# Fused Fourier mixing and maxout feed-forward: the order of the first loads, two-engine casts, a column fetched through DRAM, and where the last scatter stores are issued

## The chip, the cores and the metric

The kernel runs on one core of one Trainium2 chip. The metric is the device time of one execution in microseconds (us); the time given for the kernel is the median of several runs. A core has five engines with an instruction stream each: PE (TensorE, the matrix unit), DVE (VectorE), ACT (ScalarE), POOL (GpSimd) and SP (SyncE, which here only issues DMAs). They run side by side and wait for each other on semaphores. Matmuls write to PSUM, which is divided into banks; DVE and ACT read PSUM and copy ("evict" or "cast") its content to SBUF, where the operands of the next matmul lie. [...]

## The reference, cut to what matters

```
def _attn_ref(x):                       # x: 8 x 3072 x 256, float32
    X = np.fft.fft(x, axis=1)
    X = np.fft.fft(X, axis=2)
    return X.real

def _moe_ref(x, w1, w2, w3, w_out):     # 24576 tokens, d_model 256, d_ff 768
    h = np.maximum(np.maximum(x @ w1, x @ w2), x @ w3)
    return h @ w_out
```

The output is `_moe_ref(_attn_ref(x))`, 24576 x 256 in float32.

## The kernel before, in words

The transform along the sequence is split in two steps (one of 32 points, one of 96 points), the transform along the features is folded into the weights: tables `md` and `nmd` of cosines and sines are multiplied with the weights (`product`, L303), which gives `g_all` and, as differences, `gd_all`. Half of the feature range follows from the other half by symmetry, so each unit of work computes a "plus" and a "minus" result from the same operands.

**Stages of one batch** (class `Mix`, L383). `load_x` (L116) brings rows of x into `xt` by a DMA on POOL's queue that also casts to bf16; h = 0 is the first half of the rows, h = 1 the mirrored ones. `mirror` (L123) fills partitions 64 to 127 with the features in reverse order, on DVE for batch 0, plus one strided copy of a single column. `s(k)` (L392) is the first transform step for eight of the 49 rows (k = 6 is the last row alone) and casts the PSUM result into `tb`. For batch 0, `t` (L428) transposes `tb` into `yb` on DVE; later batches go through DRAM instead (`y`, `z`, L414 and L421, on SP). `k` (L456) is the second step; its casts give `tE` and `tO`, the operands of everything after. For block 0 of batch 0 `tE` is cast by DVE and `tO` by ACT.

**Units.** Each batch has 18 units: three blocks of 512 tokens times six column groups `jc` of d_ff. `begin` (L852) and `finish` (L869) compute one unit. A normal unit needs four matmuls and casts both halves; a "split" unit (odd ones from the 7th on, and those in `EXTRA`) has its third product computed ahead by `third` (L837): two matmuls, an ACT copy `odd`, a DVE operation `even` that adds `vb` times the column `wcol`, and on POOL two sums `plus` and `minus` (L850). DVE then takes the maxima (L862, L874). `l2_block` (L553) multiplies the hidden values with `w_out` and adds a linear part; `l2_last` (L584) does it for the last block, and stores as it goes.

**Stores.** The plus half of a block is stored by SP (`stores_plus`). The minus half goes out by indirect DMAs from POOL; they wait in the list `waiting`, and `scatter(n)` (L649) issues n of them at fixed units: one at units 8, 10 and 12 and two at unit 14, the rest at the end (L904, L919). They share POOL's queue with the sums.

**The order of the work** is written out by hand: nothing moves except by its place in the program. L672 to L725 are the head, before the first unit; `plan` (L754 to L820) gives what is put behind each unit of the main loop (L880). [...]

**What the change touches.** `FIRST` (L147) are the row ranges in which batch 0 is loaded: 0 to 16, 16 to 32, 32 to 40, 40 to 49. The loads stand behind six index ramps on POOL (L149 to L157). The cast of `s(5)` (L690) is one DVE copy. `column` (L345) makes `wcol`, one number per d_ff index, by 24 matmuls of one column and an ACT copy; it stands behind unit 5 (L797). The scatter pace is L904.

Of the kernel before, what the change touches and what calls it, by code (L numbers as in the profile page):

```python
# [9 lines left out]
FP32 = mybir.dt.float32  # L10
BF16 = mybir.dt.bfloat16
# [16 lines left out]


FIRST_OF = (4, 8, 1)  # L30
EXTRA, EXTRA_LAST = (0, 4, 8), (0, 4, 8, 14)


def _parts(g):

    done = [(12 + i - 1, slice(128 * i + 96, 128 * i + 128)) for i in range(4)]
    for i in range(4 if g < 2 else 3):
        done.append((FIRST_OF[g] + i - 1, slice(128 * i, 128 * i + 96)))
    if g == 2:
# [5 lines left out]
def kernel(  # L45
# [9 lines left out]
    nc = tc.nc  # L55

    B, S, D = x.shape
    assert (S, D) == (3072, 256)
    DFF = moe_w1.shape[1]
    NJC = DFF // 128  # L60
# [3 lines left out]
    NS = 49  # L64
# [6 lines left out]
    consts = ctx.enter_context(tc.tile_pool(name="consts", bufs=1))  # L71
    ps_f = ctx.enter_context(tc.tile_pool(name="ps_f", bufs=3, space=bass.MemoryType.PSUM))
    d_pool = ctx.enter_context(tc.tile_pool(name="dbuf", bufs=1, space=bass.MemoryType.DRAM))
    dbs = [d_pool.tile([NS, 64 * 128], BF16, name=f"db{i}", tag=f"db{i}") for i in range(2)]
    vds = [d_pool.tile([1, NHALF], BF16, name=f"vd{i}", tag=f"vd{i}") for i in range(2)]
    t_pool = ctx.enter_context(tc.tile_pool(name="tbuf", bufs=2))

    xt = [consts.tile([128, NS * 256], BF16, name=f"xt{i}", tag=f"xt{i}") for i in range(2)]
# [17 lines left out]
    md = [md_all[:, fc * 256:(fc + 1) * 256] for fc in range(2)]  # L96
    nmd = [nmd_all[:, fc * 256:(fc + 1) * 256] for fc in range(2)]
    w1_bf = consts.tile([128, 2 * DFF], BF16, tag="w1_bf")
    w2_bf = consts.tile([128, 2 * DFF], BF16, tag="w2_bf")
    w3_bf = consts.tile([128, 2 * DFF], BF16, tag="w3_bf")  # L100
    wout_bf = consts.tile([128, NJC * 256], BF16, tag="wout_bf")
    g1t = consts.tile([128, NJC * 256], BF16, tag="g1t")
    g_all = consts.tile([128, 4 * DFF], BF16, tag="g_all")
    g_all = g_all.rearrange("p (c k j) -> p c k j", k=4, j=128)
# [5 lines left out]
    mark = consts.tile([1, 1], FP32, tag="mark")  # L110
    sgn = consts.tile([128, 1], FP32, tag="sgn")
    wcol = consts.tile([128, NJC], FP32, tag="wcol")
    dif = consts.tile([128, 1], FP32, tag="dif")
    t_mid = consts.tile([128, 2, B], BF16, tag="t_mid")

    def load_x(b, s0, s1, h):  # L116

        rows = x[b].rearrange("(a s) d -> a s d", s=96)
        lo, hi = (s0, s1) if h == 0 else (max(s0, 1), min(s1, 48))
        src = rows[:, lo:hi, :] if h == 0 else rows[:, 97 - hi:97 - lo, :][:, ::-1, :]  # L120
        return nc.gpsimd.dma_start(out=xt[b % 2][32 * h:32 * h + 32, lo:hi, :], in_=src)  # L121

    def mirror(b, s0, s1):  # L123

        t = xt[b % 2]
        fn = (nc.vector.tensor_copy, (nc.gpsimd.tensor_copy, nc.vector.tensor_copy)[s0 >= 25],
              nc.scalar.copy)[min(b, 2)]
        fn(out=t[64:128, s0:s1, 1:128], in_=t[0:64, s0:s1, 255:128:-1])  # L128
        if b < 2:
            if b == 0 and s0 < 40:  # L130
                fn = nc.scalar.copy
            fn(out=t[64:128, s0:s1, 0], in_=t[0:64, s0:s1, 128])
# [8 lines left out]
    ps_s = ps_s_cm.__enter__()  # L141

    def iota(t, pattern, base=0, cm=0):
        nc.gpsimd.iota(t, pattern, base=base, channel_multiplier=cm,
                       allow_small_or_imprecise_dtypes=True)

    FIRST = ((0, 16), (16, 32), (32, 40), (40, NS))  # L147

    pidx = gen.tile([128, 1], FP32, tag="pidx")  # L149
    iota(pidx, [[0, 1]], cm=1)  # L150
    pidx_i = gen.tile([128, 1], INT32, tag="pidx_i")
# [18 lines left out]
            iota(kvec[:, NHALF:NHALF + 1], [[0, 1]], base=0)  # L170

    dvec = gen.tile([128, 128], FP32, tag="dvec")
    for c, (s0, s1) in enumerate(FIRST):
        for h in range(2):
            load_x(0, s0, s1, h)
        if c == 0:
            iota(dvec, [[1, 128]])
        elif c < 3:
            ramp(c - 1)

    def load_w(k, j0, j1):
# [74 lines left out]
    dve = nc.vector.tensor_copy  # L256
# [17 lines left out]
    def wrap(c0, c1):  # L274
# [3 lines left out]
    phase(512, 1024)  # L278
    mirror(0, *FIRST[0])
    turns(512, 1024)  # L280
    nc.vector.tensor_scalar(out=vm, in0=vm, scalar1=255, scalar2=None, op0=ALU.bitwise_and)
    nc.vector.tensor_copy(out=vm.rearrange("p (fc k c) -> p fc k c", fc=2, k=2)[:, :, :, 0],
                          in_=par.unsqueeze(1).to_broadcast([128, 2, 2]))
# [60 lines left out]

    def column():  # L345

        psc = ps_f.tile([128, 512], FP32, name="psc", tag="ps")
        for jc in range(NJC):
            for k, (table, wt) in enumerate(((md, w3_bf), (nmd, w1_bf))):
                for fc in range(2):  # L350
                    nc.tensor.matmul(psc[:, jc:jc + 1],
                                     wt[:, fc * DFF + jc * 128: fc * DFF + jc * 128 + 128],
                                     table[fc][:, 128:129],
                                     start=(k == 0 and fc == 0), stop=(k == 1 and fc == 1))
        nc.scalar.copy(out=wcol, in_=psc[:, 0:NJC])

    def prep_second():

# [290 lines left out]
    def scatter(n):  # L649

        for _ in range(min(n, len(waiting))):
            row, col, p0, p1, src = waiting.pop(0)
            stored(nc.gpsimd.indirect_dma_start(  # L653
                fours, bass.IndirectOffsetOnAxis(ap=rows_m[p0:p1, col:col + 1], axis=0),
                src, None, element_offset=256 * row), "scattered", ("scattered", "direct"))
            nc.gpsimd.memset(mark, 0.0)
# [11 lines left out]
    def warm_up(n):  # L668
        for _ in range(n):
            nc.tensor.matmul(warm, zero[:, 0:128], zero, start=True, stop=True)  # L670

    m = Mix(0)  # L672
# [8 lines left out]
    m.s(2, pool=ps_s)  # L681
    m.s(3, pool=ps_s)
    warm_up(1)
    mirror(0, *FIRST[3])
    m.s(4, pool=ps_s)
    warm_up(2)
    scal(sgn, pidx, 0.0, ALU.is_equal)
    scal(sgn, sgn, 2.0, ALU.mult, -1.0, ALU.add)
    scal(dif, sgn, 1.0, ALU.subtract)
    m.s(5, pool=ps_s, evict=dve)  # L690
    nc.scalar.activation(out=md_all, in_=vm, func=AX.Sin, scale=float(2.0 * math.pi / 256.0),
                         bias=turn[:, 0:1])
    m.s(6, pool=ps_s)
    m.t()
    warm_up(2)
# [6 lines left out]
    for (s0, s1) in HALVES:  # L702
        for h in range(2):
            load_x(1, s0, s1, h)
        if s0 == 0:
            nc.gpsimd.dma_start(out=wout_bf.rearrange("p (jc c) -> p jc c", jc=NJC),
                                in_=moe_w_out.rearrange("(jc p) c -> p jc c", jc=NJC))
# [8 lines left out]
    table(1, 512, 1024)  # L716
    m.c(1, 16)
    warm_up(1)
    m.k(0, 0, dve)
    m.k(1, 0)  # L720
    differ(0, 2, 0, 128)
    keep(psg2, 1, 2, 128, 384, dve)
    differ(0, 2, 128, 384)
# [21 lines left out]
    first, second = prep_first(), prep_second()  # L745
# [42 lines left out]
    for (u, fn) in ((0, lambda: table(2, 512, 1024)),   # L788
                    (0, lambda: next(second)), (0, lambda: next(first)),
                    (1, lambda: m.k(1, 1)), (1, lambda: next(second)), (1, lambda: next(first)),  # L790
                    (1, lambda: table(0, 512, 1024)),
                    (2, lambda: m.v(1)), (2, lambda: m.k(0, 1)), (2, lambda: next(first)),
                    (2, lambda: next(second)), (2, lambda: next(first)), (2, lambda: table(1)),
                    (3, lambda: m.c(16, RI)), (3, lambda: m.c(0, 1)),
                    (3, lambda: table(2)), (3, lambda: table(0)),
                    (4, lambda: m.k(1, 2)), (4, lambda: m.k(0, 2)), (4, m.end),
                    (5, rows), (5, column), (5, lambda: next(second)), (6, lambda: m.v(2))):  # L797
        at(0, u, fn)

    for ch in range(4):  # L800
# [79 lines left out]
    for g in range(B * UNITS):  # L880
        b, u = divmod(g, UNITS)
        blk, jc = divmod(u, NJC)
        mm = mixes[b]
        last = b == B - 1 and blk == 2
        if jc == 0:
            hp = h_pool.tile([128, NJC, TOKB], BF16, name="hp", tag="hp")
            hm = h_pool.tile([128, NJC, TOKB], BF16, name="hm", tag="hm")
            if last:
                flipped = []
                for t, name in ((mm.tE, "tEr"), (mm.tO, "tOr")):  # L890
                    fl = h_pool.tile([128, TOKB], BF16, name=name, tag=name)
                    flipped.append(fl)
                    nc.gpsimd.tensor_copy(fl, t[:, 3 * TOKB - 1: 2 * TOKB - 1: -1])
        if prev is not None and is_split(prev[0]) and not is_split(g):
            finish(*prev)
            prev = None
        pses = begin(g, hp[:, jc, :])
        if prev is not None:
            finish(*prev)
        prev = (g, pses, hm[:, jc, ::-1] if last else hm[:, jc, :])  # L900
        for lead in (1, 2):
            if is_split(g + lead) and (lead == 1) == (g + lead == 7):
                third(g + lead)
        scatter({8: 1, 10: 1, 12: 1, 14: 2}.get(u, 0))  # L904
        l2_some(10)
        if b == B - 1 and u in (1, 3):
            if u == 1:
                middle = l2_mid()
            next(middle, None)
        for fn in plan.get((b, u), ()):  # L910
            fn()
        if jc == NJC - 1:
            l2_some(1000)
            if g == B * UNITS - 1:
                finish(*prev)
            l2_queue.append(l2_last(hp, hm, mm.tE, mm.tO, flipped) if last else
                            l2_block(b, blk, hp, hm, mm.tE, mm.tO))
# [32 lines left out]
```

## Time and profile before

| what | value |
|---|---|
| median of 3 runs | 392.08 us (391.94 to 392.52) |
| the profiled execution | 391.42 us |
| span of its instructions | 389.3 us |
| mean granted TensorE clock | 0.998 |
| DMA, mean over the span | 139 GB/s |

The span runs from the first instruction to the last event of the core; 2.1 us of the profiled execution lie around it. The page has six parts: busy time by engine, the span in 40 slices, the DMA queues, the chain of work that ended last, the costliest groups, and the DMA issues. Busy time of PE counts the whole length of overlapping matmuls, so the chain and the waits, not the busy share, tell whether it is the bound. In the chain a piece stands with its start and its length, the engine, the tile and the line; in the timeline a row has start, length, engine, line, operation, output and input tiles, shape, count, and in brackets the idle time before and what ended it. Rows of the same form are merged, and "x18" is their number.

### The profile page before, as it was taken

The numbers are of one execution on the slowest core, as the hardware profiler recorded it, in microseconds if no ns is written. First come the engines' busy times: TensorE is split into PE (matmuls) and PEld (weight loads), VectorE is DVE, ScalarE is ACT, GpSimd is POOL, SyncE is SP. The second block draws the span as 40 slices with busy tenths as digits, with TensorE's granted clock in tenths as the row PEclk, the third lists the DMA queues.
The fourth block names the chain that finished last, engine by engine and source line by source line (L and its number), as shares of the span: only waits on it lengthen the run. The fifth ranks groups of instructions, "written<-read, shape, count | busy, mean of one in ns | idle before, by whom it ended". The sixth has DMA issues, their size and how long they took to land.

```text
span 389.3 us, 8092 instructions
## 1 busy us (share of the span) xinstructions
PE 376.2 (97%) x2817; PEld 236.2 (61%) x2817; DVE 327.7 (84%) x552; ACT 248.4 (64%) x453; POOL 314.3 (81%) x363
## 2 busy tenths in 40 slices
PE   6699999999999999999999999999999999999985
PEld 2355566566665666566665666656665666666654
DVE  7788797799797988899797988989887997999972
ACT  6877789567856696567856687567866346434420
POOL 9983576879898898879898898879787887769881
PEclk9999999999999999999999999999999999999999
DMA  7999764585747666475938657575423544212226
GB/s 113 184 183 160 163 145 118 112 168 161 178 141 130 172 176 154 111 128 186 189 120 149 169 151 176 125 128 185 113 94 93 149 138 139 70 31 80 85 89 206
DMA packets 52263, 54.13 MB, mean 139 GB/s; under 512 B 26547, under 2 KB 45009, under 8 KB 51367
## 3 DMA queue, kind: packets, MB, share of 16 engines
q0 software_dynamic: 20272, 26.45, 34.4%
q1 hardware_dynamic: 31418, 26.58, 25.0%
q10 hardware_dynamic: 532, 0.59, 0.5%
q8 instruction: 22, 0.36, 0.3%
q14 instruction: 19, 0.16, 0.1%
HBM read 36.95 MB, written 30.81 MB: 174 GB/s over the span
## 4 chain that ended last, share of the span: by engine, by line
PE 87%; POOL 4%; DVE 4%; DMA 2%; ACT 1%; issue 1%; DVEq 0%; POOLq 0%
PE po L549 30%; PE pse L492 10%; PE pse L860 5%; PE pse L485 5%; PE pse L486 5%; PE d L843 5%; PE e L841 5%; PE pse L861 5%; PE po L572 5%; PE ps L461 3%; PE ps L396 3%; PE pl L565 2%; DMA xt<-in_x_dram 2%; POOL xt L121 1%; POOL plus L850 1%
## 5 line engine op out<-in xcount | busy, mean ns | idle before, releaser
L850 POOL TENSOR_TENSOR plus<-even,odd 128x512 bf16<-128x512 f32 x91 | 115.7, 1271 | 55.4 <-DVE even L846 44.1
L850 POOL TENSOR_TENSOR minus<-even,odd 128x512 bf16<-128x512 f32 x91 | 115.5, 1269 | 0.0
L845 ACT ACTIVATE odd<-d 128x512 f32<-128x512 f32 x91 | 54.4, 598 | 55.8 <-PE d L843 41.9
L862 DVE SCALAR_TENSOR_TENSOR hp<-pse,plus 128x512 bf16<-128x512 f32 x91 | 62.6, 688 | 32.2 <-PE pse L861 27.9
L549 PE MATMUL po<-wout_bf,hp 128*128 128x256 bf16 x576 | 86.1, 273 | 0.0
L498 ACT ACTIVATE stmp<-pse 128x512 bf16<-128x512 f32 x106 | 63.2, 600 | 24.2 <-PE pse L486 11.2
L549 PE MATMUL po<-wout_bf,hm 128*128 128x256 bf16 x576 | 78.6, 273 | 0.0
L549 PEld LDWEIGHTS <-hp 128*128 128x128 bf16 x576 | 56.3, 98 | 26.2
L492 PE MATMUL pse<-tO,gd_all 128*128 128x512 bf16 x197 | 66.1, 380 | 1.3 <-DVE hp L862 1.3
L846 DVE SCALAR_TENSOR_TENSOR even<-vb,wcol,e 128x512 f32<-128x512 bf16 x91 | 67.1, 737 | 0.0
L549 PEld LDWEIGHTS <-hm 128*128 128x128 bf16 x576 | 56.3, 98 | 16.4
L874 DVE SCALAR_TENSOR_TENSOR hm<-pse,minus 128x512 bf16<-128x512 f32 x91 | 61.9, 680 | 0.4
L499 DVE TENSOR_TENSOR hp<-pse,stmp 128x512 bf16<-128x512 f32 x53 | 36.4, 686 | 8.8 <-ACT stmp L498 4.2
L499 DVE TENSOR_TENSOR hm<-pse,stmp 128x512 bf16<-128x512 f32 x53 | 36.5, 689 | 6.7 <-ACT stmp L498 4.3
L485 PE MATMUL pse<-tE,g_all 128*128 128x512 bf16 x106 | 40.2, 379 | 0.8 <-DVE tE L463 0.4
L577 DVE TENSOR_TENSOR kq<-po,even 128x512 f32<-128x512 f32 x60 | 40.9, 682 | 0.0
L128 ACT COPY xt<-xt 64x762 bf16<-64x762 bf16 (+1 forms) x48 | 39.8, 838 | 1.0
L486 PE MATMUL pse<-tO,g_all 128*128 128x512 bf16 x106 | 40.2, 379 | 0.0
L572 PE MATMUL po<-gw,tO 128*128 128x512 bf16 x92 | 34.9, 379 | 0.0
L860 PE MATMUL pse<-tE,g_all 128*128 128x512 bf16 x91 | 34.6, 380 | 0.1
L653 POOL DMA_INDIRECT out_dram<-kq,rows_m x29 | 29.0, 1000 | 6.8 <-issue 5.7
L841 PE MATMUL e<-tE,g_all 128*128 128x512 bf16 x91 | 34.5, 379 | 0.0
(173 smaller groups left out, 511.7 us busy)
## 6 DMA issues: line engine op xcount, KB each, us to landing
xt<-in_x_dram POOLq DMA_DIRECT2D x14, 384.0 KB
db<-tb SPq DMA_DIRECT2D x21, 192.0 KB
out_dram<-obuf SPq DMA_DIRECT2D x8, 384.0 KB
out_dram<-kq SPq DMA_DIRECT2D x8, 384.0 KB
vb<-vd SPq DMA_DIRECT2D x23, 128.0 KB
xt<-in_x_dram POOLq DMA_DIRECT2D x7, 400.0 KB
xt<-in_x_dram POOLq DMA_DIRECT2D x7, 368.0 KB
out_dram<-kq SPq DMA_DIRECT2D x7, 288.0 KB
```

The source lines that it names most:

```text
L485: nc.tensor.matmul(pse[:, 0:n], g_all[:, jc, 2 * i, :], te, start=True, stop=False)
L486: nc.tensor.matmul(pse[:, 0:n], g_all[:, jc, 2 * i + 1, :], to, start=False, stop=True)
L492: nc.tensor.matmul(pse, gd_all[:, jc, i, :], to, start=False, stop=True, skip_group_check=True)
L498: nc.scalar.activation(out=stmp[:, 0:n], in_=pses[0][:, 0:n], func=AX.Relu)
L499: nc.vector.tensor_tensor(out=dst, in0=src3, in1=stmp[:, 0:n], op=ALU.max)
L549: nc.tensor.matmul(po, hcols(jc), wout_bf[:, jc * 256:(jc + 1) * 256], start=False, stop=(jc == NJC - 1), skip_group_check=True)
L572: nc.tensor.matmul(po, to[:, cp], gw[:, 256:768], start=True, stop=True)
L845: nc.scalar.activation(out=odd3, in_=d3, func=AX.Copy, scale=-0.5)
L846: nc.vector.scalar_tensor_tensor(out=even3, in0=vb, scalar=wcol[:, jc:jc + 1], in1=e3, op0=ALU.mult, op1=ALU.add)
L850: nc.gpsimd.tensor_tensor(out=dst, in0=even3, in1=odd3, op=op)
L862: nc.vector.scalar_tensor_tensor(out=dst, in0=pse2, scalar=0.0, in1=sums[g][0], op0=ALU.max, op1=ALU.max)
L874: nc.vector.scalar_tensor_tensor(out=dst, in0=pses[0], scalar=0.0, in1=sums.pop(g)[1], op0=ALU.max, op1=ALU.max)
```

## The change

1. **x first.** The first two loads of x (rows 0 to 16) are issued before the index ramps on POOL. The last range is loaded as two, rows 40 to 45 and 45 to 49, and mirrored in two steps; the three small DVE operations for `sgn` and `dif` move ahead of these mirrors.
2. **Casts halved.** `halves` gives the first half of a cast to DVE and the second to ACT. It is used for `s(5)` and for both casts of block 0 in `k(0, 0)` and `k(1, 0)`.
3. **Column through DRAM.** The 24 matmuls and the ACT copy go. SP writes row 0 of `g_all[:, :, 3, :]` to DRAM behind unit 3, reads it back behind unit 4, one element per partition and column, and POOL casts it to `wcol` behind unit 5.
4. **Scatter pace.** In the last batch the two scatter stores of unit 14 are issued at unit 16.

```diff
+PACE, PACE_LAST = {8: 1, 10: 1, 12: 1, 14: 2}, {8: 1, 10: 1, 12: 1, 16: 2}
...
-    FIRST = ((0, 16), (16, 32), (32, 40), (40, NS))
+    FIRST = ((0, 16), (16, 32), (32, 40), (40, 45), (45, NS))
+    def load_first(c):
+        for h in range(2):
+            load_x(0, *FIRST[c], h)
+    load_first(0)
     pidx = gen.tile([128, 1], FP32, tag="pidx")
...
-    for c, (s0, s1) in enumerate(FIRST):
-        for h in range(2):
-            load_x(0, s0, s1, h)
-        if c == 0:
-            iota(dvec, [[1, 128]])
-        elif c < 3:
+    iota(dvec, [[1, 128]])
+    for c in range(1, 5):
+        load_first(c)
+        if c < 3:
             ramp(c - 1)
...
     def column():
-        psc = ps_f.tile([128, 512], FP32, name="psc", tag="ps")
-        for jc in range(NJC):
-            for k, (table, wt) in enumerate(((md, w3_bf), (nmd, w1_bf))):
-                for fc in range(2):
-                    nc.tensor.matmul(psc[:, jc:jc + 1],
-                                     wt[:, fc * DFF + jc * 128: fc * DFF + jc * 128 + 128],
-                                     table[fc][:, 128:129],
-                                     start=(k == 0 and fc == 0), stop=(k == 1 and fc == 1))
-        nc.scalar.copy(out=wcol, in_=psc[:, 0:NJC])
+        nc.sync.dma_start(out=wd.rearrange("o (c j) -> o c j", j=128), in_=g_all[0:1, :, 3, :])
+    def column_read():
+        nc.sync.dma_start(out=wcol_b, in_=wd.rearrange("o (c j) -> j (o c)", j=128))
+    def column_done():
+        nc.gpsimd.tensor_copy(wcol, wcol_b)
...
-    mirror(0, *FIRST[3])
-    m.s(4, pool=ps_s)
-    warm_up(2)
     scal(sgn, pidx, 0.0, ALU.is_equal)
     scal(sgn, sgn, 2.0, ALU.mult, -1.0, ALU.add)
     scal(dif, sgn, 1.0, ALU.subtract)
-    m.s(5, pool=ps_s, evict=dve)
+    mirror(0, *FIRST[3])
+    mirror(0, *FIRST[4])
+    m.s(4, pool=ps_s)
+    warm_up(2)
     nc.scalar.activation(out=md_all, in_=vm, func=AX.Sin, scale=float(2.0 * math.pi / 256.0),
                          bias=turn[:, 0:1])
+    def halves(out, in_):
+        n = out.shape[-1] // 2
+        if len(out.shape) == 4:
+            n = 2
+            dve(out=out[:, :, 0:n, :], in_=in_[:, :, 0:n, :])
+            nc.scalar.copy(out=out[:, :, n:, :], in_=in_[:, :, n:, :])
+        else:
+            dve(out=out[:, 0:n], in_=in_[:, 0:n])
+            nc.scalar.copy(out=out[:, n:], in_=in_[:, n:])
+    m.s(5, pool=ps_s, evict=halves)
...
-    m.k(0, 0, dve)
-    m.k(1, 0)
+    m.k(0, 0, halves)
+    m.k(1, 0, halves)
...
-                    (5, rows), (5, column), (5, lambda: next(second)), (6, lambda: m.v(2))):
+                    (3, column), (4, column_read), (5, column_done), (5, rows), (5, lambda: next(second)), (6, lambda: m.v(2))):
...
-        scatter({8: 1, 10: 1, 12: 1, 14: 2}.get(u, 0))
+        scatter((PACE if b < B - 1 else PACE_LAST).get(u, 0))
```

More of the change, by code (lines that the diff above doesn't have):

```diff
@@ L75 @@
     vds = [d_pool.tile([1, NHALF], BF16, name=f"vd{i}", tag=f"vd{i}") for i in range(2)]
+    wd = d_pool.tile([1, DFF], BF16, name="wd", tag="wd")
     t_pool = ctx.enter_context(tc.tile_pool(name="tbuf", bufs=2))
@@ L112 @@
     wcol = consts.tile([128, NJC], FP32, tag="wcol")
+    wcol_b = consts.tile([128, NJC], BF16, tag="wcol_b")
     dif = consts.tile([128, 1], FP32, tag="dif")
```

## The prediction

> **What bounds the kernel now.** I read the page first: own time of the profiled execution, then who ended last.
>
> ```profile
> span 389.3 us, 8092 instructions
> PE 87%; POOL 4%; DVE 4%; DMA 2%; ACT 1%; issue 1%; DVEq 0%; POOLq 0%
> ```
>
> PE carries 87% of the chain. The table by stages shows where it does not:
>
> ```profile
> 100.00:340.00 240.00, 240.00 (x1832) 152.45 (x1830) 207.79 (x326) 159.12 (x289) 202.18 (x211) 1.00 0.58 143
> ```
>
> From 100 to 340 us PE never rests, and its clock is 1.00. Nothing in the change touches that stretch, so only the two ends can move the time. The chain in order of time, first the head:
>
> ```profile
> 7.22 6.05 DMA xt<-in_x_dram
> 13.37 0.55 DVE xt L128
> 14.56 0.65 DVE tb L403
> 15.31 3.77 DVE yb L429
> 19.61 0.70 DVE tE L463
> 20.36 0.38 PE pse L485
> 35.22 0.58 PE psc L351 x24
> 37.17 0.70 DVE gw L379
> 40.66 0.67 DVE even L846
> 41.46 1.27 POOL plus L850
> 45.95 0.38 PE pse L860
> ```
>
> The last rows of x land at 13.27 us, then mirror, cast, transpose and cast follow in single file until the first unit at 20.36. From 29 to 46 us DVE and ACT pieces stand between PE's; from 45.95 on the chain is PE's alone. What the head wins or loses at 45.95 is won or lost at the end. The tail:
>
> ```profile
> 366.40 0.04 DVE hm L499
> 372.77 1.12 POOL out_dram L653
> 374.19 0.98 POOL out_dram L653
> 375.26 1.25 POOL plus L850
> 376.54 0.70 DVE hp L862
> 377.28 0.38 PE pse L492
> ```
>
> Here the chain leaves PE. POOL issues two scatters, only then adds the sums of the last unit, and PE waits for the maximum made of them.
>
> **Part 4, the scatter pace.** Rows of the timeline that say what is late once the scatters are gone:
>
> ```profile
> 371.29 1.28 POOL L850 TENSOR_TENSOR minus<-even,odd 128x512 bf16<-128x512 f32 x1
> 372.60 0.74 DVE L846 SCALAR_TENSOR_TENSOR even<-vb,wcol,e 128x512 f32<-128x512 bf16 x1
> 375.05 0.68 DVE L577 TENSOR_TENSOR kq<-po,even 128x512 f32<-128x512 f32 x1
> 375.88 0.82 PE L549 MATMUL po<-wout_bf,hm 128*128 128x256 bf16 x6
> 380.00:389.30 9.30, 4.71 (x43) 3.91 (x40) 2.37 (x5) 0.00 (x0) 1.11 (x2) 0.90 0.64 204
> ```
>
> POOL is done with the sums before at 372.57, but `even` ends only at 373.34; so `plus` starts at about 373.45 instead of 375.26 and ends at 374.7. The maximum still cannot start: DVE executes in order and holds L577 until 375.73. It starts there, 0.81 earlier. PE's six matmuls before L492 start at 375.88; five more starts at 0.11 each (the chain gives 0.66 for six such matmuls) put their end at 376.54. PE therefore waits 0.74 today (377.28) and would wait for nothing. **Gain 0.74.** Everything after, the stores too, follows PE and DVE. The two scatters then stand behind the `minus` at about 376 to 378.3, and the last scatter, which began at 378.70, keeps its place within some tenths. The cost hidden here is DMA time: the last 9.3 us already run at 204 GB/s and a share of 0.64, and one of the moved stores carries 512 KB (128 partitions of 1024 float32). If the cover fails it is the third rival below.
>
> **Part 3, the column.** Rows:
>
> ```profile
> 37.17 0.69 DVE L379 CAST gw<-psw 128x512 bf16<-128x512 f32 x1 [0.28 <-PE psw L374]
> 28.53 0.48 ACT L338 CAST g_all<-psg 128x384 bf16<-128x384 f32 x1
> 29.05 0.35 SPq L470 DMA_DIRECT2D vb<-vd  x1
> 33.39 0.23 SPq L466 DMA_DIRECT2D vd<-tO  x1
> 35.79 1.38 SPq L418 DMA_DIRECT2D db<-tb  x2
> 38.13 1.41 SPq L470 DMA_DIRECT2D vb<-vd  x1
> SPq L470 <- DMA vd<-tO: 5.0, 2, 4.0
> 34.00:39.00 5.00, 5.00 (x53) 2.96 (x52) 4.15 (x9) 2.46 (x6) 0.00 (x0) 1.00 1.22 198
> ```
>
> Removed: 24 matmuls, 0.58 on the chain. But DVE waited only 0.28 for the matmuls behind them (L374); before that it was busy. So the cast of `gw` comes 0.28 earlier and no more, and what follows to 45.95 with it. **Gain 0.28** (bounds: 0 to 0.58).
>
> Added: the write cannot go before `g_all` is whole (29.01) and SP has issued `vb` (29.40). A 1 KB write of `tO` to DRAM made SP wait 4.0 us once, and the one issued at 33.39 let `vb` go at 38.13. By these two the write lands at 33.5 to 34.2. The read stands behind the second `tO` write on SP (33.6). It is 128 partitions by 6 elements, each alone: 768 pieces of 2 bytes. The `db` writes are 768 pieces of 256 B each; SP spent 1.38 on two of them, so 0.7 here, to about 34.8. Landing: no row shows such a read. [...] Upper end: the 1536 pieces of `db` went from 35.79 to 39.54 at most (the `vb` behind them held SP for 1.41 where the first took 0.35), so about 1.9 for 768, after the 4.7 that the small write at 33.39 took: 34.8 + 4.7 + 1.9 = 41.4. I take 39.5, nearest to the small write's row (34.8 + 4.7), because the share of 1.22 says the queue is full. Then POOL casts (0.2) and still has its row-index work, about 1.4, before `plus`. Today `even` needs the column at 40.66 and `plus` starts at 41.46; a landing up to 39.8 costs nothing. Queued behind the waits: on SP the `db` writes, which in any case wait until 35.79 for DVE; on POOL only the row indices, idle time today. **Cost 0**, with little room.
>
> [...]
>
> **Part 2, the halved casts.** The order of the changed kernel's instructions, with their waits, shows all three ACT halves waiting on the DVE half of the same cast. The two run one after the other. The trace has that pattern already:
>
> ```profile
> 37.89 0.47 ACT L380 ACTIVATE gw<-psw,sgn 128x256 bf16<-128x256 f32 x1 [1.90 <-DVE gw L379]
> 383.81 0.42 DVE L606 COPY kq<-po 128x256 f32<-128x256 f32 x1 [0.18 <-PE po L549]
> 19.96 0.58 ACT L463 CAST tO<-ps 128x512 bf16<-128x512 f32 x1 [0.54 <-PE ps L461]
> 14.61 0.27 ACT L411 CAST tb<-ps 64x128 bf16<-64x128 f32 x1 [0.28 <-PE ps L406]
> ```
>
> L380 reads the same PSUM tile as L379 and writes other columns, and sat idle 1.90 until DVE had finished. A DVE half costs 0.42 (L606), an ACT half between half of 0.58 and 0.47, say 0.38. For `tE`: 0.42 + 0.05 + 0.38 = 0.85 instead of 0.70. For `tO` the ACT half follows DVE's second half: PE's second operand is ready at 19.61 + 0.84 + 0.05 + 0.38 = 20.88 against 20.54 today. **Loss 0.33** at the first units, if `yb` comes when it did. For `tb` the pair takes 0.85 against 0.65, and the last row's cast (0.27), parallel today, queues behind it on ACT: 0.4 later, unless x is earlier.
>
> [...]
>
> **Part 1, x first.**
>
> ```profile
> 1.51 1.39 POOL L121 DMA_DIRECT2D xt<-in_x_dram  x2
> 15.74 0.27 POOL L442 COPY x0u<-xt 128x48 bf16<-128x48 bf16 x1
> ```
>
> The first load starts 0.67 earlier (the ramps before it ran from 0.84); the second pair does not, since the same instructions stand ahead of it. The landing of the last rows moves by between 0 and 0.67, and the split lets most of the mirror run before. But two more DMA issues (0.70 each by this row) push everything behind them on POOL, `x0u` from 15.74 to 16.9 or later; PE needs it before the last weight products and `yb`'s matmuls, and ACT, without a gap up to 14.33 (L411 idle from then), casts what comes of it before `tO` can start. The 0.4 to 0.5 that x wins is spent on the longer `tb` casts and on this. **Net 0** at `tO`, bounds a gain of 0.35 and a loss of 0.15.
>
> **Sum.** -0.74 - 0.28 + 0.33 + 0 = -0.69: 391.42 becomes 390.73 for the profiled execution. That execution is 0.66 below the median of the runs, 392.08; so I forecast 392.08 - 0.69 = **391.4**.
>
> **The rivals.**
> - *The column comes late, and the kernel is slower.* The place is `even` at 40.66, then `plus`. Each us of landing beyond 39.8 is a us. It eats the gain from 40.5 on and makes the kernel measurably slower from 42. For it: the share of 1.22 and the 4.7 of a tiny write. Against it: `db`'s pieces drained at 2.4 ns each. At a landing of 42.5, 392.08 - 0.69 + 2.7 = 394.1; at 41.0, 392.6.
> - *The head does gain.* x lands 0.67 earlier, ACT and POOL keep up, the halves cost nothing net and the first units start 0.4 earlier: -0.74 - 0.28 - 0.4 = -1.4, 390.7. For it: the chain's 6.05 of DMA. Against it: the waits of the halves, and ACT without a gap.
> - *The tail gives nothing.* The 0.6 MB of moved stores meet the last stores, the end waits for DMA instead: 0.7 lost again, 392.1. For it: 204 GB/s; against it: the share of 0.64 leaves room.
>
> **How the numbers follow.** Forecast 0.45, column late 0.18, head gains 0.25, tail nothing 0.12. Runs of this kernel can tell 0.2%, 0.8 us, from no change: faster means below 391.3, slower above 392.9. The forecast lies at that edge: of its 0.45 I put 0.17 below and 0.28 within. Faster 0.17 + 0.25 = 0.42; slower: two thirds of the late column, 0.12, and 0.05 for sizes missed elsewhere, 0.17; same 0.41. The range: the gaining head gives 390.7, and half a us beyond it the bounds of column and x (0.3 and 0.35) give 390.2; above, the late column up to a landing of 41.4, 393.0. Left out are later landings and larger gains, about 0.2. The forecast's own range is 390.9 to 391.9.
>
> **What would show it.** Tail: `plus` of the last unit at about 373 to 374 and no wait of PE for `hp` (if `hp` still waits for POOL, the step is wrong). Column: the idle time of DVE's first `even` and what ended it; POOL named there is the first rival. Halves: ACT's halves of `tE` and `tO` starting after DVE's end; starting together refutes me. x: the start of the `yb` transpose, 15.31 today, against the first unit at 20.36. A first unit before 20.2 would make the head wrong, an end more than 4.5 us after the last DVE copy the tail.

## The result, and the profile after

The changed kernel takes 396.47 us (median of 5 runs, 394.98 to 397.55) against 391.94 us for the kernel before (5 runs, 391.67 to 392.52): the ratio is 1.0109 with a 95% interval of 1.0085 to 1.0133. It is slower by about 4.5 us. The profiled execution took 394.98 us, the shortest of the five.

The page of the changed kernel: its span, the shares of the chain by engine, and the group of DVE's `even` (after the second bar its idle time and what ended it).

```profile
span 393.0 us, 8009 instructions
PE 87%; DVE 3%; DMA 2%; issue 2%; ACT 2%; POOL 2%; SPq 0%; POOLq 0%; DVEq 0%
L864 DVE SCALAR_TENSOR_TENSOR even<-vb,wcol,e 128x512 f32<-128x512 bf16 x91 | 67.2, 738 | 2.7 <-POOL wcol L361 2.7
```

PE's share of the chain is what it was. What is new is a wait of DVE for `wcol`, 2.7 us, where the kernel before had none. The chain of the changed kernel in its head, in order of time:

```profile
15.73 3.77 DVE yb L435
...
20.94 0.38 ACT tO L708
...
21.36 0.38 PE pse L492
...
34.45 8.98 DMA wcol_b<-wd
...
43.56 0.19 POOL wcol L361
...
45.12 1.27 POOL plus L868
...
49.61 0.38 PE pse L878
```

The chain enters the column's read when SP issues it, at 34.45, and leaves it 8.98 us later, at 43.43. The cast to `wcol`, POOL's row indices and the first `plus` follow. The timeline shows the waits of DVE and PE behind it:

```profile
43.79 0.75 DVE L864 SCALAR_TENSOR_TENSOR even<-vb,wcol,e 128x512 f32<-128x512 bf16 x1 [2.72 <-POOL wcol L361]
47.16 0.38 PE L498 MATMUL pse<-tO,gd_all 128*128 128x512 bf16 x1 [3.20 <-DVE hp L880]
```

And the tail of the changed kernel, POOL and the last row of DVE:

```profile
377.13 1.26 POOL L868 TENSOR_TENSOR plus<-even,odd 128x512 bf16<-128x512 f32 x1 [0.91 <-DVE even L864]
...
379.81 1.11 POOL L659 DMA_INDIRECT out_dram<-kq,rows_m  x1 [0.18 <-issue]
...
381.23 0.99 POOL L659 DMA_INDIRECT out_dram<-obuf,rows_m  x1 [0.22 <-issue]
387.67 0.42 DVE L612 COPY kq<-po 128x256 f32<-128x256 f32 x1 [0.52 <-PE po L555]
```

In the kernel before the last copy is this piece of its chain:

```profile
384.75 0.42 DVE kq L606
```

The two profiled executions side by side; their spans differ by 3.7 us:

| point | before | after | difference |
|---|---|---|---|
| `yb` transpose starts | 15.31 | 15.73 | +0.42 |
| first matmul with `tO` (PE) | 20.59 | 21.36 | +0.77 |
| first `plus` on POOL | 41.46 | 45.12 | +3.66 |
| last DVE copy ends | 385.17 | 388.09 | +2.92 |
| end of span | 389.3 | 393.0 | +3.7 |

The head lost 3.66. Between the first `plus` and the last copy 0.74 was won. Between the last copy and the end (4.13 before, 4.91 after) 0.78 was lost again in this pair of executions.

### The profile page after: what moved, and what is told of

It reads as the page before. It is cut to its first block, busy times and chain, and to the rows that moved or that the text cites. A ratio compares the mean times of both kernels' runs of the same rounds, so it can differ in the third digit from the quotient of the medians.

```text
span 393.0 us, 8009 instructions
## 1 busy us (share of the span) xinstructions
PE 373.8 (95%) x2744; PEld 236.3 (60%) x2793; DVE 329.2 (84%) x555; ACT 248.8 (63%) x454; POOL 315.8 (80%) x366
## 2 busy tenths in 40 slices
DMA packets 53123, 54.14 MB, mean 138 GB/s; under 512 B 27375, under 2 KB 45837, under 8 KB 52227
## 4 chain that ended last, share of the span: by engine, by line
PE 87%; DVE 3%; DMA 2%; issue 2%; ACT 2%; POOL 2%; SPq 0%; POOLq 0%; DVEq 0%
PE po L555 31%; PE pse L498 11%; PE pse L492 5%; PE e L859 5%; PE pse L878 5%; PE po L578 5%; PE d L861 5%; PE pse L491 5%; PE pse L879 4%; PE ps L467 3%; PE ps L402 3%; PE pl L571 3%; DMA wcol_b<-wd 2%; DVE yb L435 1%; PE psg L314 1%
## 5 line engine op out<-in xcount | busy, mean ns | idle before, releaser
L131 ACT COPY xt<-xt 64x762 bf16<-64x762 bf16 (+1 forms) x48 | 39.8, 838 | 1.1
L492 PE MATMUL pse<-tO,g_all 128*128 128x512 bf16 x98 | 37.1, 379 | 0.7 <-issue 0.2
L491 PE MATMUL pse<-tE,g_all 128*128 128x512 bf16 x97 | 36.7, 379 | 0.9 <-ACT tE L708 0.5
L861 PE MATMUL d<-tO,gd_all 128*128 128x512 bf16 x91 | 34.5, 379 | 0.1
```

The lines of the kernel that those rows point to most:

```text
L491: nc.tensor.matmul(pse[:, 0:n], g_all[:, jc, 2 * i, :], te, start=True, stop=False)
L492: nc.tensor.matmul(pse[:, 0:n], g_all[:, jc, 2 * i + 1, :], to, start=False, stop=True)
```

## The experiments

My theory after this comparison: the column's read came late and is nearly the whole loss, the tail's gain is given back to the stores, and the other two parts lose something that the late column covers. The rival: the column was late only because the first parts pushed the queues by 0.7.

### The column alone

The kernel before, with part 3 of the change and nothing else.

```diff
...
-                    (5, rows), (5, column), (5, lambda: next(second)), (6, lambda: m.v(2))):
+                    (3, column), (4, column_read), (5, column_done), (5, rows), (5, lambda: next(second)), (6, lambda: m.v(2))):
```

> The kernel before with the weight column through DRAM and nothing else. Theory A (the read itself takes some 9 us from issue to landing, whatever else is changed): issued at about 33.7 us instead of 34.45, it lands at 42 to 43, the first sums of the split unit start about 3 us later than 41.46, and the time is 394.5 to 395.5. Theory B (the read was late because the other parts of the change had pushed the queues by 0.7 us): it lands before 41 and the time is 391.7 to 392.7.

Measured: 395.53 us (6 runs) against 392.19; ratio 1.0082 (1.0065 to 1.0099). Its chain:

```profile
29.02 5.54 DMA wd<-g_all
...
34.58 7.74 DMA wcol_b<-wd
...
44.01 1.27 POOL plus L852
```

Theory A holds; the column alone costs 3.3 us. Two trips to DRAM stand one behind the other: the write of 1.5 KB takes 5.54, the read 7.74. The read is issued no earlier here than in the changed kernel, but lands at 42.32 instead of 43.43. POOL issues the four loads of x beside it 2.0 earlier as well. The first line is this run's, the second the changed kernel's:

```profile
28.59 2.59 POOL L123 DMA_DIRECT2D xt<-in_x_dram  x4
```

```profile
30.63 2.61 POOL L124 DMA_DIRECT2D xt<-in_x_dram  x4
```

So the rival has a part of it: the changed kernel's first `plus` is 1.11 later than this one. That the later loads of x are the reason was not tested by itself.

The first `plus` is 2.55 later than before, but the last copy, which ends at 389.09, is 3.92 later, and PE starts its first split unit at 49.90 against 45.95. The rest is in PE's rows and in the table by stages (start and end, then busy time and number of instructions of PE, PEld, DVE, ACT and POOL, the clock, DMA's share, GB/s), of this run:

```profile
46.05 0.50 PE L494 MATMUL pse<-tO,gd_all 128*128 128x512 bf16 x1 [2.88 <-DVE hp L864]
46.34 0.63 PE L487 MATMUL pse<-tE,g_all 128*128 128x512 bf16 x1
46.77 0.63 PE L488 MATMUL pse<-tO,g_all 128*128 128x512 bf16 x1
```

```profile
46.05:49.61 3.56, 3.56 (x13) 1.83 (x13) 3.00 (x5) 1.42 (x2) 3.00 (x5) 0.52 0.53 166
```

and the same stretch of the changed kernel's profiled execution:

```profile
46.05:49.61 3.56, 2.33 (x15) 1.46 (x15) 3.19 (x6) 1.42 (x2) 2.99 (x5) 1.00 0.46 148
```

After 2.88 us without work PE's matmuls of 512 columns start 0.43 apart, against 0.22 in the same run from 49.90 on, and the granted clock is 0.52 for 3.56 us. By these two numbers I estimate that this takes up to 3.56 x 0.48 = 1.7 from PE, and 3.92 - 2.55 = 1.37 of it is left at the last copy. A comparison is the kernel of the next section that reads half the column. PE waits nearly as long there and starts with its matmuls at the full length of 0.38, by its timeline:

```profile
46.00 0.38 PE L495 MATMUL pse<-tO,gd_all 128*128 128x512 bf16 x1 [2.74 <-DVE hp L865]
```

Its clock stays at 1.00, and its first `plus` and its last copy are late by the same amount, 2.50 and 2.47. In the profiled execution of the changed kernel PE waited 3.20 and kept its clock. Its other four executions have a mean clock of 0.993 where the profiled one has 0.996, and spans of 394.0 to 395.5 instead of 393.0. That fits a loss of clock, but no trace of them shows where it lies.

### Why the read takes so long

Two edits of the kernel with the column alone. In the first only half of the pieces are read, and each is used twice, so its output is not the reference's.

```diff
...
-        nc.sync.dma_start(out=wcol_b, in_=wd.rearrange("o (c j) -> j (o c)", j=128))
+        nc.sync.dma_start(out=wcol_b[:, 0:3], in_=wd.rearrange("o (c j) -> j (o c)", j=128)[:, 0:3])
...
```

> As the run with the column alone, but only three of the six weight columns are read from DRAM, and used twice; the output is not the reference's. 384 pieces instead of 768. Theory A (the pieces themselves take the time): the read, 7.74 us for 768 pieces, falls to 4 to 5. Theory B (the read waits for its turn behind the loads of x, few pieces or many): it stays at 7 to 9.

In the second the four loads of x for the third batch are issued two units later.

```diff
-        at(0, 4, lambda ch=ch: fetch(2, ch))
+        at(0, 6, lambda ch=ch: fetch(2, ch))
```

> As the run with the column alone, but the four loads of x for the third batch are issued two units later, so that they do not stand beside the column's write and read. Theory A (the pieces take the time): the read stays at 7 to 8 us. Theory B (it waits behind the loads of x): write and read together fall from 13.3 to some 6 to 8 us, and the sums start by 42.

The chain with half the pieces:

```profile
29.11 6.45 DMA wd<-g_all
...
35.58 6.57 DMA wcol_b<-wd
```

Timeline and a row of the stages with the loads out of the way:

```profile
34.04 0.39 SPq L353 DMA_DIRECT2D wcol_b<-wd  x1
36.88 0.19 POOL L357 CAST wcol<-wcol_b 128x6 f32<-128x6 bf16 x1 [7.65 <-DMA wcol_b<-wd]
41.47 1.27 POOL L852 TENSOR_TENSOR plus<-even,odd 128x512 bf16<-128x512 f32 x1 [2.73 <-ACT tb L402]
```

```profile
34.00:36.00 2.00, 2.00 (x14) 1.12 (x13) 1.94 (x7) 1.48 (x4) 0.00 (x0) 1.00 0.16 1
```

The first kernel, 393.87 us in its one run, does not decide. Its 6.57 lies between the ranges of the two theories. Its read was issued 1.0 later than the whole read and landed at nearly the same time, 42.15 against 42.32. So half the pieces may have saved 1.2 us, or nothing. The second kernel decides. With the loads of x out of the way, at a DMA share of 0.16, all 768 pieces (the page of the changed kernel counts 27375 packets under 512 B, that of the kernel before 26547) are there in 2.7 us: issued at 34.04, cast at 36.88, which in the other traces is 0.13 behind the landing. The first `plus` then waits for ACT until 41.47, not for the column. The write is shorter too: issued at 30.41, it has landed when SP issues the read, at most 3.6 later. So theory B holds: about 5 of the 7.74 us are waiting beside the loads of x, and the pieces are at most the 2.7. These are one execution each, and DMA times vary between executions (the write took 5.54 and 6.45 in the two kernels that have it unchanged). The second kernel took 405.22 us in its one run, for the loads it delays are needed (its chain stands in one of them for 14.60 us from 44.54). The column can be had in time or the loads can, on these queues.

How the read and the loads share the DMA engines, and whether each single piece waits for its turn, no run shows.

### The pace alone

The kernel before, with part 4 and nothing else.

```diff
+PACE, PACE_LAST = {8: 1, 10: 1, 12: 1, 14: 2}, {8: 1, 10: 1, 12: 1, 16: 2}
...
-        scatter({8: 1, 10: 1, 12: 1, 14: 2}.get(u, 0))
+        scatter((PACE if b < B - 1 else PACE_LAST).get(u, 0))
```

> The kernel before with the last batch's two scatters moved behind the last sums and nothing else. Theory A (the stores take back what PE gains): PE's wait of 0.74 for the last maximum disappears, the last copy of VectorE ends about 0.7 us earlier than 385.17, and the distance from it to the end grows by the same 0.7: the time stays at 391.9, within 0.2. Theory B (the longer drain of the changed kernel came from elsewhere): 391.2.

Measured: 392.54 (11 runs) against 392.19, ratio 1.0005 (0.9997 to 1.0014): no gain, as theory A had it. In its trace the last copy ends at 384.81, and its head was 0.38 late (first `plus` at 41.84): 0.74 is won, to the hundredth what I had forecast. From there to the end it takes 5.6 instead of 4.13, 1.5 longer where theory A had 0.7.

One pair of traces overstates this. In the eight traces of this case whose last batch has the old pace, the kernel before among them, the end follows the last copy by 4.1 to 4.8 us, 4.4 in the mean. In the three with the new pace it follows by 4.9, 5.3 and 5.6. So the new pace lengthens the end by some 0.8, about what PE gains. The stages of this run, and then of the kernel before, show where:

```profile
376.00:378.00 2.00, 2.00 (x19) 1.70 (x18) 2.00 (x5) 0.41 (x1) 1.60 (x4) 1.00 0.03 8
...
387.00:388.00 1.00, 0.00 (x0) 0.00 (x0) 0.00 (x0) 0.00 (x0) 0.00 (x0) 1.00 0.78 238
```

```profile
376.00:378.00 2.00, 1.41 (x13) 1.03 (x11) 1.46 (x3) 0.03 (x1) 1.72 (x2) 1.00 0.52 211
...
387.00:388.00 1.00, 0.00 (x0) 0.00 (x0) 0.00 (x0) 0.00 (x0) 0.00 (x0) 0.69 0.12 39
```

Before, the DMA engines moved 211 GB/s, 422 KB, from 376 to 378, behind the 512 KB scatter that POOL issues from 374.19 on, while PE computed. Now they stand nearly idle there (8 GB/s, a share of 0.03) and still move 238 GB/s at 387, when nothing else is left to do.

### What is left without the column; x first; the halves

Three kernels: the changed one with the matmul column; the kernel before with x first alone; and with x first and the halved casts.

> The changed kernel with the weight column by matmuls as before. Theory A (the first units 0.77 us later are a loss of their own, only hidden behind the late column, and the tail gives nothing): 392.6 to 392.9. Theory B (the head's delay is absorbed before the first sums at 41.46): 391.9, or 391.2 where the tail gives its 0.74 as well.

> The kernel before with x issued first, its last rows in two transfers and the small vectors and mirrors moved, whole casts, matmul column, old pace. Theory A (the order of issues costs what it wins: the ramps come 0.6 later, the last rows land no earlier): the transpose starts between 15.2 and 15.6, the time is 391.8 to 392.3. Theory B (x is worth something, and only the halves spoil it): the transpose starts at 14.9 and the time is 391.5.

> The changed kernel with the matmul column and the old pace: x first and the halved casts. Theory A (the halves add 0.3 to 0.4 at the first units to what x first costs alone, 0.5, and the new pace then gives nothing): 392.9 to 393.2, as the changed kernel with the matmul column. Theory B (the two losses lie beside each other, and the rest of that run's loss was the pace's): 392.5 to 392.7.

Measured: without the column 393.05 against 392.19, ratio 1.0028 (1.0016 to 1.0039). x first alone 392.69 against 392.19, ratio 1.0014 (1.0005 to 1.0022). x first with halves 393.00 against 392.29, ratio 1.0015 (1.0004 to 1.0027). The third comes as its theory A had it, the first 0.15 above. x first alone is slower than either theory had it, although its transpose starts earlier, at 15.15. Rows of its timeline, PE and DVE:

```profile
18.31 0.21 PE L451 MATMUL psx<-tabx,x0u 128*128 128x17 bf16 x2 [0.50 <-POOL x0u L446]
19.93 0.69 DVE L466 CAST tE<-ps 128x512 bf16<-128x512 f32 x1 [1.06 <-PE ps L464]
```

and of its chain:

```profile
17.86 0.27 POOL x0u L445
...
20.79 14.11 DMA xt<-in_x_dram
...
34.99 0.55 DVE xt L128
...
42.41 1.27 POOL plus L855
```

`x0u` comes at 17.86 instead of 15.74, PE waits 0.50 for it (the first row) in front of the weight products that precede `yb`'s matmuls, and the cast of `tE` starts at 19.93 instead of 19.61 in spite of the earlier transpose. POOL's work behind it is late by 2.1 too. That includes a load of x for the next batch, issued at 20.27 instead of 18.14, whose mirror then stands late in DVE's order (34.99 instead of 33.77), and `plus` starts at 42.41, 0.95 late.

The halves run as forecast, the DVE half and then the ACT half (in the changed kernel DVE's half of `tE` ends at 20.44 and ACT's starts at 20.48), but their price cannot be read from the medians: the intervals of x first with and without them overlap. The trace with them shows one thing more, PE and then a stage:

```profile
16.36 0.28 PE L311 MATMUL psg<-w_bf,nmd_all 128*128 128x128 bf16 x2 [1.00 <-ACT nmd_all L711]
```

```profile
18.00:20.00 2.00, 2.00 (x13) 1.42 (x11) 1.43 (x1) 1.46 (x5) 2.00 (x5) 0.50 1.20 169
```

The ACT half of `tb` pushes the table `nmd_all` back, PE waits 1.00 for it after a stretch in which it was half idle (busy 1.11 of the 2 us from 14 to 16), and in this execution its clock was 0.65 from 16 to 18 and 0.50 from 18 to 20. In the changed kernel PE had the same wait of 1.00 at the same place, behind the same 1.11 us of work from 14 to 16, and its clock stayed at 1.00. So the wait alone does not decide it.

### The halves alone

> The kernel before with the three halved casts and nothing else. Theory A (the halves run one after the other, as in the changed kernel): the transpose starts 0.4 later than 15.31, the second operand of the first unit 0.3 later again, the first units come 0.75 late and all of it stays: 392.8 to 393.1. Theory B (as predicted, 0.33 at the first units and the rest hidden): 392.5.

Measured: 393.83 (6 runs) against 391.97, ratio 1.0048 (1.0031 to 1.0065): more than either theory. The chain names the reason:

```profile
15.32 0.24 issue
15.56 0.72 ACT md_all L701
16.28 0.16 ACT tb L411
16.44 0.03 issue
16.47 3.77 DVE yb L429
```

In the kernel before `md_all` stands behind `s(5)` in ACT's order. The last row's cast for the transpose thus comes behind the ACT half, which waits for DVE, and behind `md_all` as well: the transpose starts at 16.47. The change had put `md_all` ahead of it. So this run prices the halves in another order than the change's, and says nothing of those in the change beyond the mechanism.

### Edits that the runs suggest

The column's matmuls two units earlier; the two late scatters parted; both; and early scatters instead of late ones.

The early column, and then the two paces of the last batch, parted and early; the line that uses them is that of the pace above.

```diff
...
-                    (3, lambda: table(2)), (3, lambda: table(0)),
+                    (3, lambda: table(2)), (3, lambda: table(0)), (3, column),
...
-                    (5, rows), (5, column), (5, lambda: next(second)), (6, lambda: m.v(2))):
+                    (5, rows), (5, lambda: next(second)), (6, lambda: m.v(2))):
```

```diff
+PACE, PACE_LAST = {8: 1, 10: 1, 12: 1, 14: 2}, {8: 1, 10: 1, 12: 1, 14: 1, 16: 1}
...
```

```diff
+PACE, PACE_LAST = {8: 1, 10: 1, 12: 1, 14: 2}, {8: 2, 10: 2, 14: 1}
...
```

> The kernel before with two edits drawn from the runs: the 24 matmuls of the column stand two units earlier, where PE has idle time between 30 and 34 us, and the last batch's two scatters are parted, one in its old place and one behind the last sums. Theory A (what counts in the tail is that PE does not wait and that the stores do not pile up behind it; in the head DVE's 0.28 of waiting goes): PE's wait of 0.74 before the last unit goes, the end follows the last copy by 4.1 to 4.5 us again, and the time is 391.1 to 391.5. Theory B (the drain of the stores sets the end whatever the order, and the head gives nothing): 392.0 to 392.3.

> The kernel before with the column's 24 matmuls two units earlier and nothing else, to part the two edits of the run before. Theory A (the head's 0.28 of DVE's waiting goes and no more): 391.7 to 391.8, not to be told from the kernel before. Theory B (all of that run's gain is the head's): 391.3.

> The kernel before with the last batch's two scatters parted, the small one in its old place and the 512 KB one behind the last sums, and nothing else. Theory A (PE gains 0.74 and the late 512 KB take back part of it): 391.5 to 391.8. Theory B (they take back all of it): 392.0 to 392.2.

> The kernel before with the early column, and the last batch's scatters two at the eighth unit, two at the tenth and one at the fourteenth: the 512 KB one stays where it was, and the three small ones go earlier instead of later, into idle time of POOL. Theory A (PE's two waits of 0.76 and 0.74 stand behind POOL's scatters, and stores that are early leave the drain as it was): most of both waits goes, the end follows the last copy by 4.1 to 4.5 us, 390.4 to 391.0. Theory B (the sums are later for the scatters ahead of them and PE waits there instead): 391.6 to 392.3.

| kernel | us | before | ratio (95% interval) |
|---|---|---|---|
| early column, parted scatters | 391.29 | 391.97 | 0.9980 (0.9968 to 0.9992) |
| early column alone | 391.92 | 392.29 | 0.9982 (0.9967 to 0.9996) |
| parted scatters alone | 391.82 | 392.29 | 0.9979 (0.9966 to 0.9992) |
| early column, early scatters | 391.61 | 392.29 | 0.9978 (0.9965 to 0.9991) |

All four beat both kernels, the one before by 0.4 to 0.7 us; they cannot be told from each other, and the two edits together are not measurably better than one of them. The first of the four has the time of its theory A, but not by the path that the theory gives. PE's wait before the last unit is gone, but in its trace the end follows the last copy after 5.1, not 4.1 to 4.5. The parted pace keeps part of PE's 0.74, as its theory A had it. In its trace the last copy ends at 384.40, 0.77 earlier with the head as before, and the end follows after 4.8, which is the upper edge of what the old pace shows. With early scatters the end follows as with the old pace (last copy at 384.99, end 4.5 later), but the time lies at the edge of theory B. PE still waits twice, by its timeline:

```profile
370.24 0.38 PE L493 MATMUL pse<-tO,gd_all 128*128 128x512 bf16 x1 [0.35 <-DVE hp L863]
372.70 0.38 PE L493 MATMUL pse<-tO,gd_all 128*128 128x512 bf16 x1 [0.56 <-DVE hp L863]
```

The sum, 0.91, stands against 0.76 and 0.59, so 1.35, in the timeline of the kernel before. (The 0.59 is the wait that the prediction counts as 0.74, from the end of the work by the chain.) With the early column alone DVE casts `gw` without waiting, and the first `plus` starts at 40.73 in an execution whose transpose was early too, at 14.96. The median gains 0.37, near the 0.28 of theory A. The execution of the profile keeps nothing of it: the `plus` near 70 us starts at 70.07, against 69.16 before, and the chain says why:

```profile
58.02 5.68 DMA vd<-tO
...
63.72 2.87 DMA vb<-vd
```

A 1 KB write and the read behind it make DVE and then PE wait there. What the head wins can be lost at the next such trip.

## Why the prediction was wrong

- **The step that failed** is the landing of the column, "I take 39.5, nearest to the small write's row". It was 43.43, beyond even the upper end of 41.4. The issue was as forecast: SP was done with it at 34.85. What was mis-sized is the delay behind it, 8.6 us where I took the 4.7 of one small write; with the column alone it is 7.3. The runs showed in its place a wait beside the loads of x, about 5 us of the read, which goes when they go. One row of a small write was no upper end for such a wait: the column's own write took 5.54 and 6.45 in two kernels that have it unchanged. With the loads of x out of the way, at a DMA share of 0.16, the read took 2.7 from the start of its issue. My first rival, with its price of a us for a us, was the right one: 43.43 - 39.8 = 3.6, and `plus` came 3.66 later. But what stands between the landing and `plus` is the cast and POOL's row indices, as Part 3 of the prediction had it; `even` ended at 44.54, before they did. The rival also says that the kernel is measurably slower from a landing of 42 on; by its own terms that is 41.3.
- **Missed altogether**: a loss of PE's clock. In the run with the column alone it was 0.52 for 3.56 us after a wait of 2.88, and 1.4 us of that was left at the last copy; in the changed kernel's profiled execution, after a wait of 3.20, it stayed at 1.00.
- **The column's removal**: the mechanism was right. Without the 24 matmuls `gw` is cast with no idle time ahead of it, at 36.79 in the run with the column alone and 37.17 before, 0.38 earlier (forecast 0.28). Nothing of it is left where `plus` waits for the read.
- **The scatter pace**: every sentence on PE held, the gain of 0.74 to the hundredth. "Everything after, the stores too, follows PE and DVE" did not: the stretch from the last copy to the end is some 0.8 longer. I named the cover, the DMA share of 0.64 over the last 9.3 us, and read room into a mean, while the two us after 380 already ran at 0.97. The third rival was right. An end more than 4.5 us after the last copy was no safe sign against the tail, for the old pace shows up to 4.8. I also did not see a first wait of PE, 0.76 at 372.14, for an `hp` that needs a `plus` behind another scatter in POOL's order.
- **x first**: the net of 0 was mis-sized, +0.5 as a median, beyond the bound of a 0.15 loss. The first load starts 0.25 earlier (1.26 against 1.51), not 0.67, and the pairs behind it start 0.5 to 0.6 later (the second at 3.62 against 3.08). I had `x0u` at "16.9 or later"; it came at 17.86, and I stopped at `tO`, while the loads behind it on POOL were late by 2.1 too and surfaced at 35 us.
- **Halved casts**: one after the other, as forecast, 0.35 more at the second operand in the changed kernel (0.77 against the 0.42 of the transpose; forecast 0.33), where it is covered by the column. I left out that the longer `tb` casts push `nmd_all` back and make PE wait 1.00. With that the second rival, a head that gains, was wrong in both its parts.
- **The sum**: by the single runs the parts cost +3.3 (column), +0.7 (x first and halves) and +0.35 (pace, not clear of noise), 4.4 together; the change cost 4.5. I had -0.69. That the three add up so well is partly luck, since the column's share holds a loss of clock that differs between executions and its read lands later beside the other parts.

## What to carry to other kernels

A load that replaces cheap engine work must be timed beside the transfers that are in flight with it. Here 1.5 KB took 5.5 us to write and 7.7 to read beside 1.5 MB of loads, and the second trip waited anew. When stores in a tail are moved behind the last sums, look for idle time of the DMA engines after the move, in the windows one by one and not in their mean: here their share was 0.97 from 380 to 382 before the move, PE won 0.74, and the end came some 0.8 later behind the last copy. When an issue is put first in the order of an engine, follow everything behind it until somebody waits, not only to the next milestone: here the first load started 0.25 earlier in the changed kernel, and with x first alone the first `plus` came 0.95 later.

## What the runs showed of the hardware

Two traces show PE's granted clock fall in the head. With the column alone it was 0.52 for 3.56 us, after 2.88 us idle. With x first and the halves it was 0.65 from 16 to 18 and 0.50 from 18 to 20, after a stretch that was half idle (busy 1.11 of 2 us) and ended in 1.00 us idle. It stayed at 1.00 after 3.20 us idle in the changed kernel and after 2.74 with half the column read, and also after the same 1.00 in the changed kernel. So the length of the wait does not decide it in these traces; what does is not shown.

The last rows of x, with the same head, landed at times that put the start of the transpose anywhere between 14.96 (the early column alone) and 15.95 (the early column with the parted scatters) in the profiled executions. A change of a few tenths in that head can only be seen in medians.
